# One visit of TensorE for the state products of two blocks, and a new order of seven output products

## The chip, the cores and the metric

The kernel runs on one core of a Trainium2 chip. Its time is device microseconds of one execution; of several executions the median counts. TensorE (PE) multiplies and writes its products to PSUM, which has eight banks of 128x512 float32. VectorE (DVE) and ScalarE (ACT) read the banks out, GpSimd (POOL) works on SBUF alone, and SyncE (SP) issues every DMA. PEld is the weight load that goes ahead of each matmul.

## The reference

Attention between 512 tokens and 32 state rows for 8 batches (blocks) of 8 heads, in both directions, and then two gated layers on 4608 tokens of width 512 with 1536 hidden features, all in float32:

```python
a = softmax(x @ state.T / 8);  xread = a @ state       # per block and head, D = 64
a2 = softmax(state @ x.T / 8); sread = a2 @ x
x = concat(xread, sread) as [4608, 512]
x = ((x @ w_a) * (x @ w_b)) @ w_out                    # layer 1
x = (silu(x @ w_gate) * (x @ w_val)) @ w_out2          # layer 2
```

## The kernel before

**Arithmetic.** A float32 operand is split into a high part and a rest (`hi_lo`, L355: a cast on ACT, a subtraction on DVE), and a product takes three matmuls: high by high, high by low, low by high. The attention weights `a` are not multiplied by the state first. The kernel multiplies the state by the layer's weights (`sw_here`, L512: state @ w) and then `a` by that, so a block needs state @ w for each of six column groups `fp`. One such product is a *visit*: eight matmuls of 64 rows by 32 columns (two heads in the row halves, four head pairs in the column strips), which the chip runs as sixteen records, eight at a time. Its two banks are then split into `swh` and `swl` (L526 to L529).

**Stages.** Blocks 0 to 3 start layer 1 alone or in pairs; then the pairs (0,1), (2,3), (4,5), (6,7) follow in `pair` (L803), and the rows of the states (`moe("s")`). For each feature group, `gemm` (L707, matmuls at L713) makes two products into the banks `ab0` and `ab1`; one is copied out (L344), the other multiplied onto it (L962). The product with `w_out` for a pair of blocks is done by seven products in place of eight (Winograd's scheme). Their operands are sums made on DVE (`operand_sums`), and the products 1, 2, 6, 5, 7, 4, 3 are *units*, one for each half i of the columns (`unit`, matmuls at L1120). A unit has two running banks, X for the products 1, 6, 7, 4 and Y for 2, 5, 3. After each product the running sum is copied out of its bank (`c`, added to `acc` from an earlier chunk), so the next product on that bank has to wait for the copy. In layer 1, X0 and X1 are the banks `po2` and `po3`, Y0 and Y1 are `po0` and `po1`. Layer 2 (`second`) uses the same scheme for its gate and value products (L954) and its output units; its weights are converted in the time of layer 1, kept in DRAM, and loaded again `AHEAD_US["w"]` ahead of use (tiles `wg`, `w2`, `w1`, `wv`).

**Order.** Everything is recorded as tasks (`Program.add`) with engines, an estimated cost, buffers, a due time and sometimes an earliest start. `Program.order` is a list scheduler that writes one order for all engines: a free engine takes the ready task that is due first. Tasks of `main` (the big products) carry a planned clock; the tasks on PE without one are the visits: scores `psc` (L562), transposes `pr`, `pat` and `pa` (L580, L626, L660), reads `psr` (L679, 64 records), `pst` (L694) and state @ w (L522). Visits other than the first take their banks from two spare banks, tag `pt`. Forty-four *warm* tasks fill planned gaps of PE early on. The kernel has one SP queue for every DMA. The numbers at the top (starts, leads, due times, room) set where the tasks fall.

Of the kernel before, what the change touches and what calls it, by code (L numbers as in the profile page):

```python
# [10 lines left out]
F32 = mybir.dt.float32  # L11
# [25 lines left out]

FIRST_US = 30.013
STRETCH = (1.317, 1.675)

# [3 lines left out]

LEAD = (110.0, 45.724, 24.087)
ATT = (70.0, 168.526)
# [5 lines left out]

DUE = (4.03, 14.955, 38.625, -19.901, 92.0, 5.114)

# [3 lines left out]
HERE = 6  # L58
LOAD_US = 8.393
# [12 lines left out]

SPARE_US = 0.229

RESERVE, FAR_US = {"w": 3, "h": 6, "pt": 0}, 37.297
ROOM = {"w": 41, "h": 24, "pt": 2}

# [4 lines left out]
PASS_US, HALF_PASS_US = 0.2267, 0.12  # L82
SWITCH_US = 0.2
HOP_US, PE_HOP_US = 0.25, 0.3
# [9 lines left out]
def dve(n, fast=False):  # L94
    a, b = FAST_US if fast else DVE_US
    return {"DVE": a + b * n}


# [25 lines left out]
class Program:  # L124
# [37 lines left out]
    def order(self):  # L162
# [18 lines left out]
        wire = 0.0  # L181
        shared = 0.0
        events = []

# [8 lines left out]
        while events:  # L193
# [18 lines left out]
            for e, heap in ready.items():  # L212
                if free[e] > now + 1e-9:
                    continue
                held = []
                blocked = shared > now + 1e-9 and e in ("DVE", "POOL")
                while heap:
                    item = heapq.heappop(heap)
# [22 lines left out]
                    us = t.engines[e] * (2.0 if e == "PE" and t.engines[e] < 1.0 and now < COLD_US else 1.0)  # L241
                    free[e] = end = now + us
# [30 lines left out]
class Kernel:  # L273
# [238 lines left out]
    def sw_here(self, b, fp, start):  # L512

        w, st = self.whole(b, fp, start - LOAD_US), self.own_state(b)
        banks = FIRST_BANKS if b == fp == 0 else (None, None)
        ps = [self.bank(f"sw{b}_{fp}_{h}", banks[h]) for h in range(2)]

        def fn(pe):
# [4 lines left out]

        self.pe(4 * PASS_US + SWITCH_US, fn, [st, *(buf for buf, _ in w)], ps, start=start)
        hi, lo = self.w_buf(f"swh{b}_{fp}"), self.w_buf(f"swl{b}_{fp}")
# [22 lines left out]
    def attention(self, b, start, span, by_x, by_s):  # L548
# [17 lines left out]
        for h in range(2):  # L566
# [3 lines left out]
            parts.append(self.softmax2(b, h, sT, by_s))  # L570
        self.reads(b, parts, by_s)
        return out

    def turned(self, b, h, sT, by):
# [6 lines left out]

        self.pe(0.44, turn, [sT, self.ident], [ps], by=by)
        return ps

    def softmax1(self, b, g, scores, by):
# [34 lines left out]
        if scores.psum:  # L620
# [6 lines left out]

            self.pe(0.44, turn, [sn, self.ident], [pt], **kw)
            return self.split(f"xs{nm}", pt, psum=True, **kw)
# [4 lines left out]
    def softmax2(self, b, g, sT, by):  # L634
# [20 lines left out]
        self.vec(150, second, [], [st], **kw)  # L655
        pa = self.bank(f"pa{nm}")

        def turn(pe):
            for c in range(4):
                pe.transpose(pa.t[:, c * P:(c + 1) * P], e2.t[:, c * P:(c + 1) * P], self.ident.t)  # L660

        self.pe(0.44, turn, [e2, self.ident], [pa], **kw)
        xn = self.load(self.w_buf(f"xn{nm}", F32, (1024,)), self.xn[b, g], P * 4096, start=by - 25)
        a2 = self.h_buf(f"a2{nm}")
        self.copy(lambda: a2.t, lambda: pa.t, 512, [pa], [a2], **kw)
        return a2, xn, st

    def reads(self, b, parts, by):
# [15 lines left out]

        self.pe(1.1 + SWITCH_US, fn, [t for a2, xn, _ in parts for t in (a2, xn)], [ps], **kw)
        sr = self.h_buf(f"sr{b}")
# [86 lines left out]
    def out_s_part(self, f, hs, po):  # L773
# [3 lines left out]
        self.dma(  # L777
            lambda: w.t.bitcast(F32), lambda: wt.t[:, slice(0, 8, 7) if f % 2 == 0 else slice(1, 7, 5)], [wt], [w],
            P * 4096, start=self.clock - AHEAD_US["t"] * self.stretch
# [23 lines left out]
    def pair(self, u, v, xs, ws, lo, hi):  # L803
# [37 lines left out]
        ck = dict(u=u, v=v, lo=lo, n=chunk, made=made, last=hi == NFP, step=1)  # L841
        self.units = [(ck, q, i) for q in (1, 2, 6, 5, 7, 4, 3) for i in range(2)]

    def second_weights(self, f, start):
# [19 lines left out]
        if f % 2 == 0:  # L864
            self.even = t, o
            return
        self.keep_combined(f"{f // 2}", *self.even, t, o, self.wt[f // 2])

    def keep_combined(self, nm, te, e, t, o, d):
        c3, c4 = self.combined(nm, te, e, t, o)  # L870
        for k, (buf, of), at in (
            ("e", ((te, 0), e), slice(0, 8, 7)), ("o", ((t, 0), o), slice(1, 7, 5)),
            ("3", (c3, lambda: c3.t), slice(2, 4)), ("4", (c4, lambda: c4.t), slice(4, 6))
        ):
# [24 lines left out]
    def first_combined(self, fp, wo, start):  # L899
        d, raw = self.wt1[fp], []  # L900
        for f in (2 * fp, 2 * fp + 1):
            b, of = self.h_buf(f"wof{f}"), self.wof[f]
            self.dma(lambda b=b: b.t, lambda of=of: of.t, [of], [b], P * 2048, start=start)
            raw += [b, lambda b=b: b.t]
            for slot, c in ((f % 2, slice(0, 256)), (7 - f % 2, slice(256, 512))):
                self.dma(
# [3 lines left out]
        c3, c4 = self.combined(f"f{fp}", *raw)  # L910
        for k, c, at in (("3", c3, slice(2, 4)), ("4", c4, slice(4, 6))):
            self.kept(f"wt1{k}{fp}", c, lambda c=c: c.t, d, lambda x, at=at: x[:, at], lambda t: t)
# [59 lines left out]
    def second(self, u, v, ops, xs_s, chunk):  # L972
# [3 lines left out]
        for lo in range(0, NFP, chunk):  # L976
# [60 lines left out]
            ck = dict(u=u, v=v, lo=lo, n=chunk, made=made, last=last, step=2)  # L1037
            self.units = [(ck, q, i) for q in (1, 2, 6, 5, 7, 4, 3) for i in range(2)]
            if xs_s:
# [39 lines left out]
    def unit(self):  # L1079
# [8 lines left out]
        wt = self.wt1 if ck["step"] == 1 else self.wt  # L1088
        ahead = lambda k: self.clock - AHEAD_US[k] * self.stretch
        if i == 0:  # L1090
            at = (1, 2, 6, 5, 7, 4, 3).index(q)
            if at % 2 == 0:
# [133 lines left out]
    def body(self):  # L1226
# [58 lines left out]
        for fp in range(NFP):  # L1285
# [19 lines left out]
            for f in (2 * fp, 2 * fp + 1):  # L1305
# [5 lines left out]
                if f % 2:  # L1311
                    self.keep_combined(f"f{fp}", *wo1[f - 1], *wo1[f], self.wt1[fp])
        ws, sw, xs_s = {}, {}, []
        self.acc, self.units = {}, []
        for blk, lo, hi in order:
# [10 lines left out]
            if blk == "s":  # L1326
# [15 lines left out]
                continue  # L1342
            of = {}
            for b in blk if isinstance(blk, tuple) else (blk,):
                for fp in range(lo // 2, hi // 2):
                    sw[b, fp] = self.sw(b, fp, begin[b, 2 * fp] - LEAD[2])
                of[b] = self.weights(
# [93 lines left out]
```

## Time and profile before

| | |
|---|---|
| median of 3 runs | 1413.85 us (1412.05 to 1415.42) |
| the profiled execution | 1416.01 us, its span 1414.2 us |
| PE busy | 1403.5 us, 99% of the span |
| DVE busy | 1097.2 us, 78% |
| ACT busy | 722.1 us, 51% |
| granted clock of PE | 1.00 in the mean of the span |

A busy PE does not tell how fast its stream goes: matmuls overlap, and the profile's 390 ns of one 128x512 matmul is a latency. Their starts, 0.23 us apart, are the rate. What a visit costs is read from starts too: from the last matmul before it to the first after it.

### The profile page before, as it was taken

To read this page: it belongs to the slowest core of one execution; us is meant where nothing else is said; L and a number is where in the kernel's file an instruction comes from. 1 tells how busy PE (TensorE), PEld (TensorE's weight loads), DVE (VectorE), ACT (ScalarE), POOL (GpSimd) and SP (SyncE) were. 2 spreads that over 40 slices of the span, in tenths; PEclk is the share of its full clock that TensorE was granted. 3 is DMA by queue.
4 is the path that set the end of the run, shared out by engine and by line. 5 is a ranking of instruction groups with operands and counts; after the bars stand their busy time and mean duration, and the time that the engine had idled before them with its cause. 6 is when DMAs were issued, how large, how long until landed. Compare 5 with 4: busy or idle time off the path is not lost.

```text
span 1414.2 us, 21772 instructions
## 1 busy us (share of the span) xinstructions
PE 1403.5 (99%) x7676; PEld 1120.6 (79%) x7676; DVE 1097.2 (78%) x1911; ACT 722.1 (51%) x1331; POOL 101.7 (7%) x78
## 2 busy tenths in 40 slices
PE   9999999999999999999999999999999999999998
PEld 7777777766777777899888788888888888888887
DVE  7999999998999998978787986649655595545464
ACT  7777675546565657556456633335323362333350
POOL 2222120000111011001011000000000000000000
PEclk9999999999999999999999999999999999999999
DMA  9879987977768898999998996668856686456486
GB/s 363 283 267 346 341 324 263 334 259 257 255 216 273 313 315 296 335 383 344 399 323 328 338 370 222 232 215 265 308 183 227 245 296 233 163 209 247 157 265 225
DMA packets 153932, 396.50 MB, mean 280 GB/s; under 512 B 16352, under 2 KB 20448, under 8 KB 153824
## 3 DMA queue, kind: packets, MB, share of 16 engines
q1 hardware_dynamic: 153824, 395.12, 79.5%
q8 instruction: 61, 1.00, 0.3%
q14 instruction: 47, 0.39, 0.1%
HBM read 298.06 MB, written 96.99 MB: 279 GB/s over the span
## 4 chain that ended last, share of the span: by engine, by line
PE 71%; DMA 3%; DVE 1%; ACT 1%; issue 0%; SPq 0%; DVEq 0%
PE pu L1120 24%; PE pX L954 18%; PE pC L954 9%; PE p L713 8%; PE pY L954 4%; PE p_s L713 2%; PE sw L522 1%; DMA w<-w 1%; PE po_s L789 1%; PE pvs L713 1%; PE pgs L713 1%; PE pus L1178 1%; DMA raw_o<-in_wo 1%; DMA xn<-in_xn 0%; DMA accc<-c 0%; DMA raw_v<-in_wab 0%
## 5 line engine op out<-in xcount | busy, mean ns | idle before, releaser
L1120 PE MATMUL pu<-S,wt 128*128 128x512 f32 x1932 | 472.5, 392 | 0.0
L1120 PEld LDWEIGHTS pu<-S,wt 128*128 128x128 f32 x1932 | 358.7, 188 | 98.1 <-issue 21.0
L713 PE MATMUL p<-xs,swh 128*128 128x512 f32 x768 | 242.5, 397 | 4.3 <-ACT a L344 2.0
L954 PE MATMUL pX<-x,w 128*128 128x512 f32 x864 | 219.9, 390 | 1.0 <-ACT t L344 0.5
L954 PEld LDWEIGHTS pX<-x,w 128*128 128x128 f32 x864 | 161.5, 188 | 35.6 <-ACT t L344 1.4
L713 PEld LDWEIGHTS p<-xs,swh 128*128 128x128 f32 x768 | 140.3, 188 | 53.3 <-ACT a L344 5.9
L713 PE MATMUL p<-xs,swl 128*128 128x512 f32 x384 | 149.9, 390 | 0.0
L962 DVE TENSOR_TENSOR t<-t,pC 128x512 f32<-128x512 f32 x96 | 65.9, 686 | 100.9 <-ACT t L344 87.6
L344 ACT COPY t<-pX 128x512 f32<-128x512 f32 x77 | 45.1, 586 | 101.7 <-PE pX L954 94.7
L352 DVE TENSOR_TENSOR S<-S,S 128x512 fp32r<-128x512 f32 x138 | 90.3, 694 | 3.4 <-ACT S L359 3.3
L962 DVE TENSOR_TENSOR c<-c,pu 128x512 f32<-128x512 f32 x102 | 69.6, 685 | 24.9 <-PE pu L1120 18.2
L344 ACT COPY a<-p 128x512 f32<-128x512 f32 x77 | 45.2, 587 | 84.7 <-PE p L713 53.8
L359 ACT CAST S<-S 128x512 fp32r<-128x512 f32 x138 | 78.9, 622 | 13.1 <-DVE S L962 5.4
L713 PEld LDWEIGHTS p<-xs,swl 128*128 128x128 f32 x384 | 72.1, 188 | 15.7
L962 DVE TENSOR_TENSOR c<-acc,pu 128x512 f32<-128x512 f32 x80 | 54.8, 686 | 28.8 <-PE pu L1120 22.8
L954 PE MATMUL pC<-x,w 128*128 128x512 f32 x288 | 73.1, 389 | 0.0
L954 PE MATMUL pX<-x,wg 128*128 128x512 f32 x282 | 71.7, 390 | 0.0
L954 PE MATMUL pC<-x,wv 128*128 128x512 f32 x282 | 71.6, 389 | 0.0
L954 PE MATMUL pY<-x,wg 128*128 128x512 f32 x282 | 71.6, 389 | 0.0
L968 ACT ACTIVATE c<-c 128x512 f32<-128x512 f32 x48 | 30.3, 631 | 72.8 <-DVE c L962 72.7
L359 ACT CAST swh<-sw 128x512 fp32r<-128x512 f32 x96 | 51.7, 589 | 28.9 <-PE sw L522 20.5
L352 DVE TENSOR_TENSOR swl<-sw,swh 128x512 fp32r<-128x512 f32 x96 | 61.8, 684 | 5.6 <-ACT swh L359 4.6
(203 smaller groups left out, 2132.1 us busy)
## 6 DMA issues: line engine op xcount, KB each, us to landing
wt<-wt SPq DMA_DIRECT2D x154, 512.0 KB, 6.3
w<-w SPq DMA_DIRECT2D x118, 512.0 KB, 6.4
wg<-w2g SPq DMA_DIRECT2D x47, 512.0 KB, 5.5
w1l<-wf SPq DMA_DIRECT2D x72, 256.0 KB, 5.1
accc<-c SPq DMA_DIRECT2D x72, 256.0 KB, 4.1
acc<-accc SPq DMA_DIRECT2D x72, 256.0 KB, 5.4
raw_w<-in_wab SPq DMA_DIRECT2D x24, 512.0 KB, 6.5
wt<-wt SPq DMA_DIRECT2D x46, 256.0 KB, 5.1
```

The lines of the kernel that those rows point to most:

```text
L344: self.nc.scalar.copy(out(), in_())
L352: lambda e: self.by_engine[e].tensor_tensor(out=out(), in0=in0(), in1=in1(), op=ALU.subtract), r, w, **kw
L359: self.p.add(act(n), lambda e: self.nc.scalar.copy(hi(), src()), [src_buf], [hb], **kw)
L522: pe.matmul(ps[h].t[cs], lhsT=st.t[rows, cs], rhs=of()[rows], start=True, stop=True)
L713: pe.matmul(ps.t[:, :n], lhsT=l, rhs=r, start=i == 0, stop=i == last)
L789: pe.matmul(ps.t[:, c], lhsT=w.t[:, k, hw, lc], rhs=hs.t[:, hh, :ST], start=f == i == j % 2 == 0, stop=f == NF - 1 and i == 2, skip_group_ ...
L954: pe.matmul(ps.t, lhsT=w.t[:, half, hw, i * P:(i + 1) * P], rhs=x.t[:, hx], start=start and i == n == 0, stop=stop and i == 1 and n == 2, ...
L962: self.vec(512, lambda e: e.tensor_tensor(out=to(), in0=a(), in1=b(), op=op), r, [w], **kw)
L968: self.p.add(act(n), lambda e: self.nc.scalar.activation(out=out.t[:, :n], in_=ps.t[:, :n], func=AF.Silu), [ps], [out])
L1120: pe.matmul(ps.t, lhsT=w.t[:, half, hw, c], rhs=x.t[:, hx], start=starts and k == m == 0, stop=stops and k == n - 1 and m == 2, skip_group ...
L1178: pe.matmul(ps.t, lhsT=h.t[:, hh, c], rhs=w.t[:, :, hw], start=k == m == 0, stop=k == len(hs) - 1 and m == 2)
```

## The change

The two blocks of a pair get state @ w in one PE task (`sw_both`), with four banks: two spare ones, and `po0` and `po1`. To free these, layer 1's units are ordered 1, 6, 7, 4, 2, 5, 3 and Y uses the same banks as X. The slots of the output weights in DRAM follow that order. The transposes `pa` of both parities (heads 0 and 1 of a pair) become one task. The scheduler prices the first visit after a main task, holds a lone visit back, and lets other visits that are due within 60 us join one that runs. Some twenty constants differ, among them the lead of layer 2's weights (21.73 to 12), the start of their conversion and the room for buffers.

```diff
-FIRST_US = 30.013
-STRETCH = (1.317, 1.675)
+FIRST_US = 31.986
+STRETCH = (1.318, 1.8)
...
-LEAD = (110.0, 45.724, 24.087)
+LEAD = (69.954, 54.422, 17.786)
...
-DUE = (4.03, 14.955, 38.625, -19.901, 92.0, 5.114)
+DUE = (5.0, 14.955, 40.0, -30.0, 40.0, 2.853)
...
-NEXT_US = 134.259
+NEXT_US = 119.329
...
-STAGGER = 40
-FROM_US = 252.5
-DIRECT = 11
-PACE = 1.062
-COMBOS = (75.0, 15.0)
+STAGGER = 49.629
+FROM_US = 305.45
+DIRECT = 12
+PACE = 0.909
+COMBOS = (100.0, 17.68)
 HELD = 4
-AHEAD_US = {"t": 18.453, "s": 10.342, "acc": 5.741, "w": 21.73, "x": 35.19}
+AHEAD_US = {"t": 17.835, "s": 10.054, "acc": 5.741, "w": 12, "x": 40}
...
-ROOM = {"w": 41, "h": 24, "pt": 2}
+ROOM = {"w": 40, "h": 26, "pt": 2}
...
-SWITCH_US = 0.2
+SWITCH_US, VISIT_US, JOIN_US, HOLD_US = 0.14, 0.2, 60.0, 10.0
...
+ORDER = {1: (1, 6, 7, 4, 2, 5, 3), 2: (1, 2, 6, 5, 7, 4, 3)}
...
+                join = [
+                    q for q in heap if not (q[2].main or q[2].spare or q[2].engine is not None) and q[2].by < main + JOIN_US
+                ] if e == "PE" else []
+                join.sort(reverse=True)
+                alone = len(join) == 1 and not visiting
...
+                    if e == "PE" and alone and not (t.main or t.spare) and t.by > main + HOLD_US:
+                        held.append(item)
+                        continue
...
+    def sw_both(self, u, v, fp, start):
+
+        w, st = self.whole(u, fp, start - LOAD_US), [self.own_state(b) for b in (u, v)]
+        ps = [[self.bank(f"sw{b}_{fp}_{h}", h if b == v else None) for h in range(2)] for b in (u, v)]
+        parts = [self.state_products(s, w, p) for s, p in zip(st, ps)]
+
+        def fn(pe):
+            for part in parts:
+                part(pe)
+
+        self.pe(
+            8 * PASS_US + SWITCH_US, fn, [*st, *(buf for buf, _ in w)], [p for pair in ps for p in pair], start=start
+        )
+        return [self.sw_split(b, fp, p) for b, p in zip((u, v), ps)]
...
-        pa = self.bank(f"pa{nm}")
...
+    def turned2(self, b, parts, by):
+        pa = [self.bank(f"pa{b}_{g}") for g in range(2)]
...
-        half = (0, 1, 0, 1, 0, 1, 0)[(1, 2, 6, 5, 7, 4, 3).index(q)]
+        half = at % 2
         if q in (1, 2, 5):
             tag = f"X{i}" if q == 1 else f"Y{i}"
-            po = 2 + i if q == 1 else i if ck["step"] == 1 else None
+            po = 2 + i if q == 1 or ck["step"] == 1 else None
...
-        if q == 7:
+        if q == (5 if ck["step"] == 1 else 7):
...
+            for fp in range(lo // 2, hi // 2):
+                if isinstance(blk, tuple) and fp < HERE and (lo or fp):
+                    sw[blk[0], fp], sw[blk[1], fp] = self.sw_both(*blk, fp, begin[blk[0], 2 * fp] - LEAD[2])
+                    continue
+                for b in blk if isinstance(blk, tuple) else (blk,):
+                    sw[b, fp] = self.sw(b, fp, begin[b, 2 * fp] - LEAD[2])
```

The built programs show what this does to PE's order. The first place is state @ w of the column group 4 for the pair (2,3) (`sw2_4`, `sw3_4`; `p0_` are the main products, `pu1_` the units). Before, block 3 on PE:

```order
L713 MATMUL p0_2_9_1_3299<-xs2_1_855,swl2_4_3225 128x512
L522 MATMUL sw3_4_0_3316<-w1l2_4_0_2855,strt3_312 32x512
L522 MATMUL sw3_4_1_3317<-w1l2_4_0_2855,strt3_312 32x512
L522 MATMUL sw3_4_0_3316<-w1l2_4_1_2861,strt3_312 32x512
L522 MATMUL sw3_4_1_3317<-w1l2_4_1_2861,strt3_312 32x512
L522 MATMUL sw3_4_0_3316<-w1l2_4_2_2872,strt3_312 32x512
L522 MATMUL sw3_4_1_3317<-w1l2_4_2_2872,strt3_312 32x512
L522 MATMUL sw3_4_0_3316<-w1l2_4_3_2875,strt3_312 32x512
L522 MATMUL sw3_4_1_3317<-w1l2_4_3_2875,strt3_312 32x512
L1120 MATMUL pu1_0_4_2_0_3331<-S1_0_4_2_0_3185,wt1_0_4_1_4_3105 128x512 x3
```

It stands by itself; block 2's eight came 42 main matmuls earlier. After, on PE, the end of block 2's part and all of block 3's:

```order
L570 MATMUL sw2_4_0_3180<-w1l2_4_3_2989,strt2_284 32x512
L570 MATMUL sw2_4_1_3181<-w1l2_4_3_2989,strt2_284 32x512
L570 MATMUL sw3_4_0_3182<-w1l2_4_0_2930,strt3_329 32x512
L570 MATMUL sw3_4_1_3183<-w1l2_4_0_2930,strt3_329 32x512
L570 MATMUL sw3_4_0_3182<-w1l2_4_1_2936,strt3_329 32x512
L570 MATMUL sw3_4_1_3183<-w1l2_4_1_2936,strt3_329 32x512
L570 MATMUL sw3_4_0_3182<-w1l2_4_2_2939,strt3_329 32x512
L570 MATMUL sw3_4_1_3183<-w1l2_4_2_2939,strt3_329 32x512
L570 MATMUL sw3_4_0_3182<-w1l2_4_3_2989,strt3_329 32x512
L570 MATMUL sw3_4_1_3183<-w1l2_4_3_2989,strt3_329 32x512
L771 MATMUL p0_1_11_1_3207<-xs1_0_472,swh1_5_3001 128x512 x2
```

The two blocks follow each other with no main matmul between. The second place is the units of the pair (0,1), chunk 4. `S1_0_4_6_0` is the operand of product 6, and the two names that begin with `pu1_0_4_1` are X0 and X1. PE before:

```order
L1120 MATMUL pu1_0_4_2_0_3331<-S1_0_4_2_0_3185,wt1_0_4_1_4_3105 128x512 x3
L1120 MATMUL pu1_0_4_2_0_3331<-S1_0_4_2_1_3193,wt1_0_4_1_5_3160 128x512 x3
L1120 MATMUL pu1_0_4_2_1_3349<-S1_0_4_2_0_3185,wt1_0_4_1_4_3105 128x512 x3
L1120 MATMUL pu1_0_4_2_1_3349<-S1_0_4_2_1_3193,wt1_0_4_1_5_3160 128x512 x3
L1120 MATMUL pu1_0_4_1_0_3227<-S1_0_4_6_0_3234,wt1_0_4_6_4_3122 128x512 x3
L1120 MATMUL pu1_0_4_1_0_3227<-S1_0_4_6_1_3256,wt1_0_4_6_5_3173 128x512 x3
L713 MATMUL p0_3_8_0_3383<-xs3_0_953,swh3_4_3344 128x512 x2
```

Product 2 on its own bank stands between the products 1 and 6 of X0. PE after, at the products 6 and 7:

```order
L1179 MATMUL pu1_0_4_1_0_3345<-S1_0_4_6_0_3244,wt1_0_4_1_4_3260 128x512 x3
L1179 MATMUL pu1_0_4_1_0_3345<-S1_0_4_6_1_3274,wt1_0_4_1_5_3293 128x512 x3
L1179 MATMUL pu1_0_4_1_1_3359<-S1_0_4_6_0_3244,wt1_0_4_1_4_3260 128x512 x3
L1179 MATMUL pu1_0_4_1_1_3359<-S1_0_4_6_1_3274,wt1_0_4_1_5_3293 128x512 x3
L1179 MATMUL pu1_0_4_1_0_3345<-S1_0_4_7_0_3270,wt1_0_4_7_4_3326 128x512 x3
L1179 MATMUL pu1_0_4_1_0_3345<-S1_0_4_7_1_3308,wt1_0_4_7_5_3342 128x512 x3
L1179 MATMUL pu1_0_4_1_1_3359<-S1_0_4_7_0_3270,wt1_0_4_7_4_3326 128x512 x3
L1179 MATMUL pu1_0_4_1_1_3359<-S1_0_4_7_1_3308,wt1_0_4_7_5_3342 128x512 x3
```

X0 comes again after one unit of six matmuls on X1.

## Rows read from the trace of the kernel before

**Rows 1.** The page's head: span; busy time of each engine.
```profile
span 1414.2 us, 21772 instructions
PE 1403.5 (99%) x7676; PEld 1120.6 (79%) x7676; DVE 1097.2 (78%) x1911; ACT 722.1 (51%) x1331; POOL 101.7 (7%) x78
```
**Rows 2.** Waits of PE: total us, times, longest; first and last listed.
```profile
PE p L713 <- ACT a L344: 2.0, 3, 1.2
...
PE p L713 <- DVE ve L962: 0.3, 1, 0.3
```
**Rows 3.** Windows: busy us of PE, PEld, DVE, ACT, POOL; clock; DMA share, GB/s.
```profile
250.00:350.00 100.00, 96.33 (x573) 68.69 (x572) 91.22 (x171) 52.24 (x99) 2.81 (x2) 1.00 0.82 280
350.00:650.00 300.00, 299.59 (x1880) 233.73 (x1879) 275.05 (x493) 183.28 (x346) 32.81 (x23) 1.00 0.86 299
```
**Rows 4.** Groups by line: state @ w, its two forms.
```profile
L522 PE MATMUL sw<-w1l,strt 64*32 64x512 f32 x576 | 40.1, 601 | 0.0
L522 PE MATMUL sw<-cv_w,strt 64*32 64x512 f32 x192 | 13.2, 601 | 0.0
```
**Rows 5.** Timeline of PE, one visit: start us, us, what.
```profile
292.05 0.62 PE L713 MATMUL p<-xs,swh 128*128 128x512 f32 x2
292.52 0.39 PE L713 MATMUL p<-xs,swl 128*128 128x512 f32 x1
292.83 1.09 PE L522 MATMUL sw<-w1l,strt 64*32 64x512 f32 x16
293.85 0.72 PE L713 MATMUL p<-xs,swh 128*128 128x512 f32 x2
294.42 0.40 PE L713 MATMUL p<-xs,swl 128*128 128x512 f32 x1
```
**Rows 6.** Timeline of PE, reads of one block, then of two together.
```profile
127.56 1.10 PE L679 MATMUL psr<-xn,a 128*32 128x64 f32 x64
128.59 0.73 PE L713 MATMUL p<-xs,swh 128*128 128x512 f32 x2
...
167.51 1.99 PE L679 MATMUL psr<-xn,a 128*32 128x64 f32 x128
169.44 0.33 PE L694 MATMUL pst<-ident,sr 128*128 128x128 f32 x1
```
**Rows 7.** Timeline of PEld: the weight loads of the visit in Rows 5.
```profile
292.83 0.18 PEld L522 LDWEIGHTS sw<-w1l,strt 64*32 64x32 f32 x16 [0.36 <-issue]
```
**Rows 8.** Timeline of DVE: the rests of that visit's banks.
```profile
297.32 1.29 DVE L352 TENSOR_TENSOR swl<-sw,swh 128x512 fp32r<-128x512 f32 x2 [1.96 <-ACT swh L359]
```
**Rows 9.** Timeline: PE's first matmul behind a unit, DVE's copy of it; three times.
```profile
229.57 0.62 PE L713 MATMUL p<-xs,swh 128*128 128x512 f32 x2
229.77 0.69 DVE L962 TENSOR_TENSOR c<-acc,pu 128x512 f32<-128x512 f32 x1
...
268.71 0.70 PE L713 MATMUL p<-xs,swh 128*128 128x512 f32 x2
...
270.99 0.65 DVE L962 TENSOR_TENSOR c<-acc,pu 128x512 f32<-128x512 f32 x1
...
298.08 0.61 PE L713 MATMUL p<-xs,swh 128*128 128x512 f32 x2
...
302.60 0.69 DVE L962 TENSOR_TENSOR c<-acc,pu 128x512 f32<-128x512 f32 x1
```
**Rows 10.** Timeline of DVE: a reduction of the softmax.
```profile
267.34 0.68 DVE L609 TENSOR_REDUCE sm<-sn 128x16 f32<-128x512 f32 x1
```
**Rows 11.** Gate weights: first issue (SP), first use (PE), landing from 650 to 690.
```profile
657.50 0.33 SPq L333 DMA_DIRECT2D wg<-w2g  x1
...
671.32 1.55 PE L954 MATMUL pX<-x,wg 128*128 128x512 f32 x6
...
DMA to landing us min/median/max: 6.1/8.1/10.0
```
**Rows 12.** The page's DMA issues: bytes of one, median us to landing.
```profile
w<-w SPq DMA_DIRECT2D x118, 512.0 KB, 6.4
```

More of the change, by code (lines that the diff above doesn't have):

```diff
@@ L96, in dve @@
     return {"DVE": a + b * n}
+ORDER = {1: (1, 6, 7, 4, 2, 5, 3), 2: (1, 2, 6, 5, 7, 4, 3)}
+SLOTS = {
+    k: {"e": slice(0, 8, 7), "o": slice(o.index(2), 7, o.index(3) - o.index(2)),
+        "3": slice(o.index(6), o.index(5) + 1, o.index(5) - o.index(6)),
+        "4": slice(o.index(7), o.index(4) + 1, o.index(4) - o.index(7))}
+    for k, o in ORDER.items()
+}
 class Buf:
@@ L182, in order @@
         shared = 0.0
+        visiting = False
         events = []
@@ L216, in order @@
                 blocked = shared > now + 1e-9 and e in ("DVE", "POOL")
-                while heap:
-                    item = heapq.heappop(heap)
+                join = [
[3 more added lines that the diff above has]
+                alone = len(join) == 1 and not visiting
+                if not visiting:
+                    join = []
+                while heap:
+                    if join:
+                        item = join.pop()
+                        heap.remove(item)
+                        heapq.heapify(heap)
+                    else:
+                        item = heapq.heappop(heap)
                     t = item[2]
@@ L241, in order @@
                     us = t.engines[e] * (2.0 if e == "PE" and t.engines[e] < 1.0 and now < COLD_US else 1.0)
+                    if e == "PE":
+                        visit = not (t.main or t.spare)
+                        us += VISIT_US * (visit and not visiting)
+                        visiting = visit
                     free[e] = end = now + us
@@ L516, in sw_here, with state_products @@
         ps = [self.bank(f"sw{b}_{fp}_{h}", banks[h]) for h in range(2)]
+        self.pe(4 * PASS_US + SWITCH_US, self.state_products(st, w, ps), [st, *(buf for buf, _ in w)], ps, start=start)
+        return self.sw_split(b, fp, ps)
+    def sw_both(self, u, v, fp, start):
[9 more added lines that the diff above has]
+        return [self.sw_split(b, fp, p) for b, p in zip((u, v), ps)]
+    def state_products(self, st, w, ps):
         def fn(pe):
@@ L522, in fn, with sw_split @@
                     pe.matmul(ps[h].t[cs], lhsT=st.t[rows, cs], rhs=of()[rows], start=True, stop=True)
-        self.pe(4 * PASS_US + SWITCH_US, fn, [st, *(buf for buf, _ in w)], ps, start=start)
+        return fn
+    def sw_split(self, b, fp, ps):
         hi, lo = self.w_buf(f"swh{b}_{fp}"), self.w_buf(f"swl{b}_{fp}")
@@ L570, in attention @@
             parts.append(self.softmax2(b, h, sT, by_s))
-        self.reads(b, parts, by_s)
+        self.reads(b, self.turned2(b, parts, by_s), by_s)
         return out
@@ L580, in turn @@
                 pe.transpose(ps.t[:, r], sT.t[:, r], self.ident.t)
-        self.pe(0.44, turn, [sT, self.ident], [ps], by=by)
+        self.pe(0.4, turn, [sT, self.ident], [ps], by=by)
         return ps
@@ L626, in turn @@
                     pe.transpose(pt.t[:, r], sn.t[:, r], self.ident.t)
-            self.pe(0.44, turn, [sn, self.ident], [pt], **kw)
+            self.pe(0.4, turn, [sn, self.ident], [pt], **kw)
             return self.split(f"xs{nm}", pt, psum=True, **kw)
@@ L655, in softmax2 @@
         self.vec(150, second, [], [st], **kw)
-        pa = self.bank(f"pa{nm}")
+        xn = self.load(self.w_buf(f"xn{nm}", F32, (1024,)), self.xn[b, g], P * 4096, start=by - 25)
+        return e2, xn, st
+    def turned2(self, b, parts, by):
+        pa = [self.bank(f"pa{b}_{g}") for g in range(2)]
         def turn(pe):
[L659 to L666, printed above, removed]
+            for (e2, _, _), ps in zip(parts, pa):
+                for c in range(4):
+                    r = slice(c * P, (c + 1) * P)
+                    pe.transpose(ps.t[:, r], e2.t[:, r], self.ident.t)
+        self.pe(0.8, turn, [self.ident, *(e2 for e2, _, _ in parts)], pa, by=by)
+        out = []
+        for g, (ps, (_, xn, st)) in enumerate(zip(pa, parts)):
+            a2 = self.h_buf(f"a2{b}_{g}")
+            self.copy(lambda a2=a2: a2.t, lambda ps=ps: ps.t, 512, [ps], [a2], by=by)
+            out.append((a2, xn, st))
+        return out
     def reads(self, b, parts, by):
@@ L683, in fn @@
                         )
-        self.pe(1.1 + SWITCH_US, fn, [t for a2, xn, _ in parts for t in (a2, xn)], [ps], **kw)
+        self.pe(0.88 + SWITCH_US, fn, [t for a2, xn, _ in parts for t in (a2, xn)], [ps], **kw)
         sr = self.h_buf(f"sr{b}")
@@ L777, in out_s_part @@
         self.dma(
-            lambda: w.t.bitcast(F32), lambda: wt.t[:, slice(0, 8, 7) if f % 2 == 0 else slice(1, 7, 5)], [wt], [w],
+            lambda: w.t.bitcast(F32), lambda: wt.t[:, SLOTS[1]["eo"[f % 2]]], [wt], [w],
             P * 4096, start=self.clock - AHEAD_US["t"] * self.stretch
@@ L841, in pair @@
         ck = dict(u=u, v=v, lo=lo, n=chunk, made=made, last=hi == NFP, step=1)
-        self.units = [(ck, q, i) for q in (1, 2, 6, 5, 7, 4, 3) for i in range(2)]
+        self.units = [(ck, q, i) for q in ORDER[1] for i in range(2)]
     def second_weights(self, f, start):
@@ L904, in first_combined @@
             raw += [b, lambda b=b: b.t]
-            for slot, c in ((f % 2, slice(0, 256)), (7 - f % 2, slice(256, 512))):
+            at = SLOTS[1]["eo"[f % 2]]
+            for slot, c in ((at.start, slice(0, 256)), (at.stop - 1, slice(256, 512))):
                 self.dma(
@@ L1037, in second @@
             ck = dict(u=u, v=v, lo=lo, n=chunk, made=made, last=last, step=2)
-            self.units = [(ck, q, i) for q in (1, 2, 6, 5, 7, 4, 3) for i in range(2)]
+            self.units = [(ck, q, i) for q in ORDER[2] for i in range(2)]
             if xs_s:
@@ L1089, in unit @@
         ahead = lambda k: self.clock - AHEAD_US[k] * self.stretch
+        at = ORDER[ck["step"]].index(q)
         if i == 0:
-            at = (1, 2, 6, 5, 7, 4, 3).index(q)
             if at % 2 == 0:
```

18 lines of the change are left out of this document (8 added, 10 removed).

## The prediction, written before the changed kernel was run

> **What bounds the kernel now.** I read the page's head, PE's waits, the stretches, and then the timeline of PE at single visits. The head shows PE busy for 1403.5 of 1414.2 us, DVE next with 78% [rows 1]. A busy PE could still be slow, so the waits come second: six, 4.9 us in all without the one at the start, the largest group 2.0 us and the smallest 0.3 us, all behind copies and sums of ACT and DVE [rows 2]. PE's stream thus sets the end, and what leaves it shortens the kernel unless a new wait stands in its place. The candidate for that is DVE: 91.2 of 100 us from 250 to 350 us, 275.1 of 300 from 350 to 650 [rows 3], which is where the changed part lies. The first of these is also the stretch in which PE was idle most, 3.7 us.
>
> Both programs hold the same matmuls; DVE has three rows fewer of 1913. What differs is how often PE leaves its main stream, and how closely one order follows another.
>
> **Merged visits.** State @ w has 768 records [rows 4], sixteen to a visit, so 48 visits. One stands in rows 5. Two main matmuls start 0.47 us apart over two steps (292.05 to 292.52), so one step is 0.235. From the last main start before the visit to the first after it is 293.85 - 292.52 = 1.33. The two matmuls behind it then take 294.42 - 293.85 = 0.57 where 0.47 is usual, 0.10 more. The visit costs 1.33 - 0.235 + 0.10 = 1.20 us.
>
> What a second block adds inside the same visit is not in the trace. The sixteen records last 1.09 us together and 0.60 each [rows 4, 5], so the last starts 0.49 after the first; eight records start within some 0.04, which leaves 0.45 from one set of eight to the next. Two more sets are 0.90. The nearest row that shows a doubled visit agrees: the reads of one block occupy PE from 127.56 to 128.59, 1.03 us, those of two from 167.51 to 169.44, 1.93 us, again 0.90 for the second [rows 6]. So a merge saves 1.20 - 0.90 = 0.30 us. The bounds are nothing (two full visits after all) and the 0.30 itself, since sets cannot come closer than in rows 5; I take 0.30. The built program has 19 merged visits and 10 single ones: 19 x 0.30 = **-5.7 us**.
>
> The loads of the second block's states are part of that price. All sixteen loads of a visit stand within 0.18 us of its start [rows 7], while its first eight matmuls run until 0.60, so the loads of the second eight went in under matmuls of the same row halves. The Trainium skill, "TensorE: Matmul & The Clock Gate", section Part 3 on row and column tiling, says that a weight load overlaps matmuls in flight only where the row group differs; by it each merge would pay 0.18 again and the term would be 19 x 0.12 = -2.3 us. The trace shows otherwise for this form, so I stay with the row.
>
> **Other visits.** In PE's order 82 visits become 61: 19 by these merges, one by the transposes, one in the start-up, among warm matmuls. Seven of the eight blocks had both transposes `pa` side by side already. The one that is new is worth 0.3 at most; I count nothing.
>
> **Slack behind a visit.** The rests of the visit in rows 5 were done at 297.32 + 1.29 = 298.61, 4.8 us after PE left it [rows 8]. Counting PE's rows by their durations, the first reader of `swl` followed a visit by less than 4 us at 10 of 48 places before, and at 3 after; the median goes from 4.5 to 6.0 us. The transposes' readers move from 1.4 to 2.7 us at three blocks. This should give back part of the 4.9 us of waits; ends 0 and -4.9, and I take **-1.5**. The four banks of a merged visit have to be split by ACT and DVE as before, no more of them in all.
>
> **Banks that come back sooner.** This is the price of the new unit order. A unit may not start on X or Y until the running sum is copied out. Counted the same way, layer 1 has 72 such returns; before, the closest came 4.1 us behind the end of the last unit on its bank and 6 came within 6 us; now four come after 1.36 us (one unit of six steps), three after 2.7, two after 3.8, and 26 within 6. The copy is done 230.46 - 229.57 = 0.9 us behind the unit where DVE is free, 271.64 - 268.71 = 2.9 us where it is behind, and 303.29 - 298.08 = 5.2 us at worst shown [rows 9]. At 0.9 no return waits. At 2.9 the four nearest wait 1.54 each and the next three 0.2: 6.9 us. At 5.2 four wait 3.8, three 2.5, two 1.4 and some 12 more up to a microsecond: about 35 us, and behind a waiting unit stands everything else on PE. In DVE's new order the copies of the closest group (products 6 and 7) have mostly one other instruction between them, such as a reduction of 0.68 us [rows 10]: with the copy 1.37 against the 1.36 of a unit, just in step, plus two short ones. Nearest is the case of 0.9; for the short ones and a late start at two places I take **+1.5**, ends 0 and +35.
>
> **Layer 2's weights.** Their lead falls from 21.73 to 12. In the built list the first gate weights stand 6.5 us of PE work ahead of use before and 2.2 after, the second 5.2 and 2.7. In the trace the first were issued at 657.50 and used at 671.32, 13.8 us ahead, and landing there took 8.1 us in the median, 10.0 at worst [rows 11]. With 4.3 us less, 9.5 us are left: enough for the median, 0.5 short at worst. I take **+0.5**, ends 0 and +4 (four loads, each 1 us late). Later on some 12 us of plan stand against 6.4 us of landing [rows 12]; no wait.
>
> **The rest.** The number of warm matmuls is the same, and two more of them stand ahead of the first main product (60 for 58), so the start-up counts nothing, with 2 us either way for its other order. The last unit and its output are unchanged.
>
> Sum: -5.7 - 1.5 + 1.5 + 0.5 = -5.2 us. The profiled execution took 1416.0 us, of it 1414.2 in the span, and lies 2.2 above the median of 1413.85. So 1416.0 - 5.2 = 1410.8 for an execution like the profiled one, and **1408.6** for the median.
>
> **Rivals.**
>
> *The returns wait (slower).* The new order puts PE behind DVE's copies of the running sums, at the group of products 6 and 7 of pair (0,1) and at pair (2,3)'s first chunk. If these copies come 3.5 us behind their units, between the 2.9 and the 5.2 of rows 9, four returns wait 2.14 and three 0.8: 10.9 us in place of 1.5. The sum is then +4.2 and the time 1418. It decides from a copy 2.9 us late, where it cancels the gain. For it: both rows of late copies stem from that very chunk, in the stretch with DVE at 91% [rows 3]. Against it: DVE's order now has the copies directly behind the units.
>
> *DVE sets the pace (no change).* All merges lie in the time of layer 1, where DVE has 92% [rows 3]. If its work and not PE's decided there, the 5.7 us would turn into waits and the time stay at 1413.9. Against it: 24.9 us of DVE were idle from 350 to 650, and PE waited less than 0.5 there. The Trainium skill says on this, in "TensorEngine Tiling (Array Packing)", section PSUM Bottleneck, that tiling speeds up TensorE but not the evacuation of PSUM, so that the copies may become the bottleneck; the rows above show DVE near it but not at it.
>
> *Late weights (no change).* The loads at the start of layer 2 cost the upper end, 4 us, in place of 0.5: -1.7, 1412.1.
>
> *The waits go as well (faster).* The looser splits remove all of the 4.9 us of waits, with 0.10 for the slower second step behind each of six, and no new ones come: -5.7 - 5.5 = -11.2, 1402.6.
>
> **How the numbers follow.** What a measurement can tell here is about 0.2%, 2.8 us: faster is below 1411.0, slower above 1416.7. The forecast has 0.50 (its own range 1405 to 1411), the waits that go 0.12: faster 0.62. DVE's pace 0.12 and the late weights 0.10: no change 0.22. The returns 0.16: slower. The range runs from 1402, which takes in most of the faster rival, to 1417, the nearer part of the slower one.
>
> **What would show it.** In the changed kernel's profile, a visit of 32 records of state @ w should take some 1.99 us, 2.23 between main starts, with 61 runs of visits; 2.4 from main start to main start or more says that merging saves little. Waits of `pu` on a copy `c` near 270 us tell the returns, waits of `pX` or `pY` on `wg`, `w2` or `w1` near 660 us the late weights; both together should stay under 2 us. Waits of `p` should fall below 4.9 us. The prediction is wrong if PE's waits grow by more than they lost in visits.

## The result and the profile after

The changed kernel takes 1402.33 us in the median of six runs (1401.76 to 1404.10), the kernel before 1414.31 in the same comparison: ratio 0.9918, 95% interval 0.9906 to 0.9931, or 12.0 us less. The forecast was 5.2 us less; the time is the one that the rival *the waits go as well* gave. The head and PE's waits after:

```profile
span 1402.2 us, 21751 instructions
PE 1392.5 (99%) x7676; PEld 1125.2 (80%) x7676; DVE 1095.8 (78%) x1908; ACT 722.6 (52%) x1334; POOL 101.9 (7%) x78
```

```profile
PE p L771 <- ACT a L373: 1.9, 1, 1.9
PE warm L1299 <- POOL ident masks.py:199: 1.4, 1, 1.4
PE sw L570 <- DVE swl L381: 1.1, 1, 1.1
PE p L771 <- DVE U L1021: 0.6, 1, 0.6
PE pX L1013 <- ACT t L373: 0.4, 1, 0.4
PE pst L752 <- ACT sr L747: 0.2, 1, 0.2
```

The span is 12.0 us shorter and PE's busy time 11.0 [rows 1]: part of that is visits, part delays that a busy PE hides. The waits without the start's are 4.2 us, hardly less than the 4.9 of before [rows 2]. The list misleads here: 1.3 of the 4.2 stand inside visits (`sw`, `pst`), and a wait is listed from a matmul's modelled end, 0.39 us after its start, while the next could have started after 0.23, so each is 0.16 longer than it reads. I therefore added up the distances from start to start on PE, by what stood there. Of a difference of 12.1 us, 5.4 are at the visits with the step behind them (92.0 to 86.6; 6.4 to 6.9 once the waits inside visits are taken out, 0.6 to 1.1 before and 2.1 after, by where one draws the line), 6.2 are delays between main matmuls (3.9 of them in *late steps*, more than 0.13 us late, whose sum went from 7.3 to 3.4; 1.1 in the second step behind each, 0.11 slower, at 13 places before and 3 after; the rest in small ones), and 0.5 at warm matmuls. The windows tell where the second part lies: PE's busy time from 250 to 350 us went from 96.33 [rows 3] to 99.79.

```profile
250.00:350.00 100.00, 99.79 (x675) 73.74 (x674) 98.39 (x182) 52.20 (x100) 5.41 (x4) 1.00 0.91 322
350.00:650.00 300.00, 297.48 (x1840) 239.28 (x1839) 274.02 (x492) 185.83 (x351) 31.30 (x22) 1.00 0.89 314
```

A merged visit on PE (start, duration, what), and its weight loads:

```profile
322.70 1.32 PE L1179 MATMUL pu<-S,wt 128*128 128x512 f32 x5
323.95 1.95 PE L570 MATMUL sw<-w1l,strt 64*32 64x512 f32 x32
325.83 0.74 PE L771 MATMUL p<-xs,swh 128*128 128x512 f32 x2
326.41 0.40 PE L771 MATMUL p<-xs,swl 128*128 128x512 f32 x1
```

```profile
323.95 0.18 PEld L570 LDWEIGHTS sw<-w1l,strt 64*32 64x32 f32 x16 [0.36 <-issue]
324.41 0.15 PEld L570 LDWEIGHTS sw<-w1l,strt 64*32 64x32 f32 x8 [0.28 <-issue]
324.84 0.15 PEld L570 LDWEIGHTS sw<-w1l,strt 64*32 64x32 f32 x8 [0.28 <-issue]
```

From its first record to the next main matmul it takes 1.88 us (325.83 - 323.95), where a visit of 16 records takes 1.02 [rows 5]. Over all undisturbed visits, counted as in the prediction from start to start with the slower step behind, the median is 2.079 us for a merged one and 1.219 for a single one, so a merge saves 2 x 1.219 - 2.079 = 0.36, and 19 of them 6.8 us.

### The profile page after: what moved, and what is told of

Same layout as the page of the kernel before. It is cut to its first block, busy times and chain, and to the rows that moved or that the text cites. A ratio compares the mean times of both kernels' runs of the same rounds, so it can differ in the third digit from the quotient of the medians.

```text
span 1402.2 us, 21751 instructions
## 1 busy us (share of the span) xinstructions
PE 1392.5 (99%) x7676; PEld 1125.2 (80%) x7676; DVE 1095.8 (78%) x1908; ACT 722.6 (52%) x1334; POOL 101.9 (7%) x78
## 4 chain that ended last, share of the span: by engine, by line
PE 72%; DMA 2%; DVE 1%; ACT 1%; issue 0%; SPq 0%; ACTq 0%; DVEq 0%
PE pu L1179 24%; PE pX L1013 18%; PE pC L1013 9%; PE p L771 7%; PE pY L1013 5%; PE p_s L771 2%; PE sw L570 1%; PE po_s L847 1%; PE pvs L771 1%; PE pgs L771 1%; PE pus L1237 1%; DMA raw_v<-in_wab 1%; DMA raw_g<-in_wab 1%; DMA w2g<-w2g 1%; DMA w1l<-wf 0%; ACT sg L447 0%
## 5 line engine op out<-in xcount | busy, mean ns | idle before, releaser
L373 ACT COPY a<-p 128x512 f32<-128x512 f32 x82 | 48.2, 588 | 88.2 <-PE p L771 85.7
L1027 ACT ACTIVATE gv<-pX 128x512 f32<-128x512 f32 x48 | 28.7, 598 | 69.4 <-PE pX L1013 69.3
L381 DVE TENSOR_TENSOR S<-U,S 128x512 fp32r<-128x512 f32 x92 | 60.8, 695 | 3.6 <-ACT S L388 3.4
```

The source lines that it names most:

```text
L373: self.nc.scalar.copy(out(), in_())
L381: lambda e: self.by_engine[e].tensor_tensor(out=out(), in0=in0(), in1=in1(), op=ALU.subtract), r, w, **kw
L1027: self.p.add(act(n), lambda e: self.nc.scalar.activation(out=out.t[:, :n], in_=ps.t[:, :n], func=AF.Silu), [ps], [out])
```

## The experiments

Each number is the median, and the ratio to the kernel before that ran beside it (its median was 1412.6 to 1414.2); 0.001 is 1.4 us. Four theories: *slack* (waits went because merged visits leave more time), *order* (because of the products' new order), *numbers* (because of the retuned numbers, above all when layer 2's weights are converted), and *fit* (numbers are tuned to one order, and any other order has other waits).

**First: parts of the change.** No merged visits:

```diff
-if isinstance(blk, tuple) and fp < HERE and (lo or fp):
+if isinstance(blk, tuple) and False:
```

> The changed kernel with no merged visits: each block's state @ w is its own visit again; the new order of products, the banks, the joined transposes and the new numbers stay. Measured so far: before 1414.3, changed 1402.3; PE's start-to-start times put 5.7 of the 12.0 us at the visits and 6.2 at waits that are gone. All theories: the visits cost some 5.7 us again. Slack (the waits went because the rests of a merged visit are split with more time to spare): the waits come back too, 1414. Numbers (they went because the retuned numbers move the conversions and loads out of 250 to 350 us) and order (they went because of the new order of the products, which changes what stands in DVE's queue ahead of an eviction): the waits stay away, 1408, and waits of p stay under 3 us.

1412.97, ratio 1.0000 (0.9990 to 1.0010): 11.6 us lost, more than the 6.8 of the visits. By the total this is what *slack* expects. The trace speaks against it: PE's waits of `p`, which *slack* said would come back, stay away.

```profile
PE sw L570 <- DVE swl L381: 1.9, 1, 1.9
PE warm L1299 <- POOL ident masks.py:199: 1.4, 1, 1.4
PE pX L1013 <- ACT t L373: 1.3, 1, 1.3
PE pu L1179 <- DMA wt<-wt: 0.8, 2, 0.7
PE p L771 <- ACT a L373: 0.6, 1, 0.6
```

Its late steps add up to 2.8 us, the changed kernel's to 3.4. What its profiled execution lost, 8.2 us of span, stands at the visits: their price, and waits in front of them. One visit PE enters 2.1 us late, on PE's timeline:

```profile
94.75 0.40 PE L771 MATMUL p<-xs,swl 128*128 128x512 f32 x1
97.09 1.68 PE L570 MATMUL sw<-w1l,strt 64*32 64x512 f32 x16 [1.95 <-DVE swl L381]
98.71 0.50 PE L771 MATMUL p<-xs,swh 128*128 128x512 f32 x1
```

It waits for the split `swl` of an earlier visit, which still holds a spare bank; three more visits, near 195, 245 and 289 us, run 0.4 to 0.7 over.

All fourteen numbers of before in the changed kernel, and all fourteen new ones in the kernel before:

```diff
-FROM_US = 305.45
+FROM_US = 252.5
...
-ROOM = {"w": 40, "h": 26, "pt": 2}
+ROOM = {"w": 41, "h": 24, "pt": 2}
```

> The changed kernel with the fourteen numbers of before that it also had (leads, due times, start and pace of the conversions, buffers): merged visits, order of products and joined transposes stay. Slack and order: 1402 to 1403, as the changed kernel. Numbers: the merges keep their 5.7 us and the waits come back, 1408.5, with more than 4 us of waits of p and pX between 250 and 350 us.

> The kernel before with the fourteen numbers of the changed kernel and nothing else. Slack and order: 1414, as before. Numbers: the waits go, the visits stay, 1408.

The changed kernel with the old numbers: 1427.43, ratio 1.0099 (1.0083 to 1.0116), 14 us *slower* than before, with late steps of 18.9 us in all, at unlike places. No theory gave this: with the old numbers the new structure is a loss. The kernel before with the new numbers: 1411.00, ratio 0.9988 (0.9979 to 0.9996). Its late steps fall from 7.3 to 3.4 us, as *numbers* expects, but its visits take 1.8 us more than before, and the total falls short of the 1408 that it expected.

Without merges and with the old order of the products (the edit also takes back the banks of Y and the merges):

```diff
...
-ORDER = {1: (1, 6, 7, 4, 2, 5, 3), 2: (1, 2, 6, 5, 7, 4, 3)}
+ORDER = {1: (1, 2, 6, 5, 7, 4, 3), 2: (1, 2, 6, 5, 7, 4, 3)}
...
```

> The changed kernel without merged visits and with the old order of the seven products and Y in banks 0 and 1 again: what is left of the change is the numbers, the joined transposes and the planner's rule of joining. Slack and order: 1414. Numbers: 1408. Against the run without merges alone it tells what the order does by itself: equal by the theory of the numbers, 6 us slower by that of the order.

1410.02, ratio 0.9981 (0.9971 to 0.9991): 2.7 us faster than with the new order. So the order does not remove waits; *order* falls. By itself, without merges, it is no gain.

**Second: how much is fit, and is it slack?** A number moved by a meaningless amount, in the changed kernel and in the run without merges; and a longer lead for single visits:

```diff
-FROM_US = 305.45
+FROM_US = 304.45
```

> The changed kernel with one number moved by a meaningless amount: the conversions start at 304.45 in place of 305.45 us of plan. The planner's greedy order comes out otherwise in hundreds of places, the structure is the same. Slack (merged visits leave few waits whatever the details): 1402 to 1404, ratio to before 0.992 as the changed kernel. Fit (the numbers were searched for this one order, and its few waits are that search's): some waits come back, 1405 to 1410, ratio 0.994 to 0.998, PE's stalls over the changed kernel's 3.4 us, at places with nothing in common.

> The run without merged visits, with the same meaningless nudge. Slack: 1413 again, 11 us behind the nudged changed kernel. Fit: anywhere from 1409 to 1417, and only about 6 us behind the nudged changed kernel, which is what the visits are worth.

```diff
-LEAD = (69.954, 54.422, 17.786)
+LEAD = (69.954, 54.422, 24.087)
```

> The run without merged visits, with each visit planned 24.1 us ahead of its weights' first use, as before, in place of 17.8. Slack: if single visits lacked time behind them, this gives it back: waits of sw and p on swl and evictions go, 1408. Fit: no such return, 1410 to 1416.

In this order: 1405.01, ratio 0.9938 (0.9925 to 0.9951); 1414.78, 1.0006 (0.9996 to 1.0016); 1414.99, 1.0008 (1.0000 to 1.0017). One microsecond in one number cost the changed kernel 2.8 us: that much of the 12.0 belongs to this one order. The longer lead gave nothing back, and without merges the waits of `p` stayed away (0.6 us, and 1.4 in its nudged twin), so *slack*, my reason in the prediction, falls. Undoing the merges costs 11.6 us, and 9.6 between the nudged twins; some 4 of the mean are lost beside the visits' own price. In the first of these runs 2.1 came where a single visit waits for the spare bank of another, and the rest I did not test.

**Third: the conversions alone.** Their planned start, end and pace, moved in the kernel before and moved back in the changed one, each with a nudged twin (start 1 us earlier):

```diff
-NEXT_US = 134.259
+NEXT_US = 119.329
-FROM_US = 252.5
+FROM_US = 305.45
-PACE = 1.062
+PACE = 0.909
```

> The kernel before, with the conversions of layer 2's weights planned as in the changed kernel (start 305.45 for 252.5 us, end and pace too) and all else as before. In before's trace PE stalls 4.6 us between 290 and 346 us, where ACT and DVE waited up to 5 us for loads. Numbers: with the conversions' loads out of that stretch these stalls go, 1409. Slack, order and fit: no gain beyond 1.5 us, or other stalls elsewhere, 1411 to 1417.

> The kernel before with the conversions' start at 251.5 in place of 252.5 us of plan. Numbers: 1412 to 1417, its waits between 290 and 346 us still there. Fit: anywhere from 1409 to 1418; at 1410 or less the gain of the late conversions would be no more than a lucky order.

> The kernel before with the late conversions, start at 304.45 in place of 305.45 us of plan. Numbers: 1408 to 1412, under the kernel before by 2 us or more. Fit: 1409 to 1418.

> The changed kernel with the conversions of layer 2's weights planned as before (start 252.5 us, end and pace of before) and all else as changed. Late conversions gave 4.4 us in the kernel before. Numbers, as a term of its own: the same 4.4 us are lost here, 1406.7, ratio to before 0.995. Fit: 1405 to 1412, no fixed sum. Slack: 1403.

> The run before this one with the start at 251.5 in place of 252.5 us of plan, a meaningless nudge. Numbers: within 3 us of that run, and both behind the changed kernel and its nudged twin. Fit: the four lie mixed.

| ratio to before | early conversions | late conversions |
|---|---|---|
| kernel before | 1 | 0.9969 (0.9957 to 0.9981) |
| its nudged twin | 0.9999 (0.9990 to 1.0007) | 0.9978 (0.9968 to 0.9989) |
| changed kernel | 0.9958 (0.9943 to 0.9973) | 0.9918 (0.9906 to 0.9931) |
| its nudged twin | 0.9962 (0.9947 to 0.9977) | 0.9938 (0.9925 to 0.9951) |

This is the answer, as *numbers* said in all five runs. By the means of the twins, late conversions give 0.0026 (3.7 us) in the old structure and 0.0032 (4.5 us) in the new one, each known to some 2 us by the intervals. The late steps agree: 7.3 and 6.4 us (twin) with early conversions and 2.6 and 2.5 with late ones in the old structure, 5.4 and 4.4 against 3.4 and 3.8 in the new one. All else of the change gives 0.0040 (5.6 us) with early and 0.0046 (6.4 us) with late conversions. That is near the 6.8 of the merged visits, but as a sum: the merges are worth 10.6 by the means of the two pairs above, so the rest of the change takes some 4 back. The two parts add up to 10.1 us, and the changed kernel's own order lies 1.4 better than its mean with its twin. Which of the three numbers does it was not separated, and with all fourteen the kernel before gains less than with these three. In the trace of the kernel before with late conversions, PE's waits and the window (busy 98.85 for 96.33 [rows 3]):

```profile
PE warm L1240 <- POOL ident masks.py:199: 1.4, 1, 1.4
PE p L713 <- DVE V L962: 1.2, 1, 1.2
PE p L713 <- ACT a L344: 0.5, 2, 0.4
```

```profile
250.00:350.00 100.00, 98.85 (x606) 71.60 (x604) 95.80 (x179) 52.70 (x99) 2.87 (x2) 1.00 0.79 268
```

**Fourth: how an early conversion costs PE anything.** The largest stall left in the changed kernel suggests a way, first on PE, then on ACT:

```profile
470.00 0.39 PE L771 MATMUL p<-xs,swl 128*128 128x512 f32 x1
472.28 0.72 PE L771 MATMUL p<-xs,swh 128*128 128x512 f32 x2 [1.90 <-ACT a L373]
```

```profile
465.54 2.03 ACT L388 CAST swh<-sw 128x512 fp32r<-128x512 f32 x4
469.92 0.66 ACT L432 ACTIVATE cv_g<-raw_g 128x512 f32<-128x512 f32 x1 [2.35 <-DMA raw_g<-in_wab]
470.49 0.76 ACT L447 ACTIVATE sg<-raw_g 128x512 f16<-128x512 f32 x1
471.12 0.64 ACT L435 ACTIVATE cv_g<-raw_g 128x512 int32<-128x512 uint32 x1
471.66 0.57 ACT L373 COPY a<-p 128x512 f32<-128x512 f32 x1
```

ACT stands for 2.35 us before a step that reads a raw load, two more conversion steps follow, and only then comes the copy `a` that frees PE's bank. The plan reckons with 2.2 us + 512 KB at 3.6e5 bytes per us = 3.7 us until such a load has landed; in this trace it takes 6.6 to 7.0 us in the median, from 300 to 650 us. So these steps stand too early in the queue: call this *queue*. The tests are known landings, in the kernel before and in the changed one with early conversions; more small buffers in the kernel before, against the rival that buffer slots are what is short (*slots*); and a still later start (340 us) in the changed kernel:

```diff
-end = max(wire, end) + DMA_US
+end = max(wire, end) + DMA_US + (3.5 if any(b.name[:5] in ("raw_g", "raw_v", "raw_o") for b in t.bufs) else 0)
```

> The kernel before, whose planner now reckons with 3.5 us more until a load of layer 2's raw weights has landed (the trace has 6 to 7 us, the plan 3.7), so that the steps reading it stand later in ACT's queue; the loads are issued as before. Queue (ACT stands still for these loads with evictions behind it): ACT's waits for raw loads go, PE's stalls from 290 to 346 us shrink, 1409 to 1410.5, ratio 0.997. Slots or traffic: 1412 to 1415.

> The changed kernel with the early conversions (1407.9, ratio 0.996), and the same 3.5 us more reckoned with. Queue: back to 1403 to 1405, ratio 0.993. Slots or traffic: 1407 to 1409.

```diff
-ROOM = {"w": 41, "h": 24, "pt": 2}
+ROOM = {"w": 40, "h": 26, "pt": 2}
```

> The kernel before with 40 large and 26 small buffers, as the changed kernel has, in place of 41 and 24. Slots (ACT waits up to 5 us for a small buffer that a store still reads): those waits shorten and PE's stalls near 302 to 314 us go, 1409 to 1411. Queue or traffic: 1412 to 1415.

> The changed kernel with the conversions from 340 us of plan on in place of 305.45. If early conversions cost by crowding the time before 350 us, most is gained already: 1401 to 1404. If each one costs wherever it stands closer together, the rest of layer 1 gets denser and it is slower: 1404 to 1408. Fit alone: 1403 to 1408.

The edit does what it is meant to do: from 250 to 650 us ACT's waits for raw loads fall from 25.5 us to 0.2 in the changed kernel with early conversions, and from 9.8 to nothing in the kernel before. The first went to 1403.70, ratio 0.9937 (0.9925 to 0.9950), as *queue* said: 0.0021 back, 3.0 us, though a nudge moves as much and this run has no twin. The kernel before became slower, 1416.05, 1.0026 (1.0015 to 1.0037), a miss by the total. In the stretch at issue 4.6 us of late steps from 290 to 346 became 0.3, and the window is full. But the last output weights of layer 2 are stored later (issued at 804.4 us for 796.9), and the start of layer 2 now waits for such weights:

```profile
250.00:350.00 100.00, 99.84 (x612) 72.82 (x611) 96.58 (x176) 58.40 (x109) 7.50 (x5) 1.00 0.89 310
```

```profile
PE pu L1120 <- DMA wt<-wt: 3.2, 2, 2.3
```

More slots: 1411.63, ratio 0.9992 (0.9984 to 1.0001), between what *slots* and its rivals said, and no clear gain. The stalls from 290 to 346 went here too, and others came (2.4 us in a visit at 117 us). The waits of ACT, then of DVE, in the kernel before from 285 to 346 us: stores that still read a small buffer, and loads of `acc`, came before raw loads:

```profile
ACT a L344 <- DMA x<-c: 8.3, 2, 5.0
ACT a L344 <- DVE c L962: 5.1, 1, 5.1
```

```profile
DVE c L962 <- DMA acc<-accc: 2.4, 1, 2.4
DVE swl L352 <- ACT swh L359: 2.4, 2, 2.0
```

Three different edits took most or all of the 4.6 us out of that stretch: 1.3 were left with late conversions, 0.3 with known landings and none with more slots, where the nudge alone left 4.3. So no single wait can be named as the cause; which of them an early conversion sets off in the kernel before stays open. Later still: 1406.76, ratio 0.9961 (0.9948 to 0.9975), 0.0043 or 6 us worse than the changed kernel. In its trace are 2.0 us of `pX` on `wg` at 813 us. That fits conversions that end late: their last step on ACT starts at 779.8 us for 769.5. The rest is spread over other late steps, or not seen in that execution.

**Last: both prices at once.** The known landings in the changed kernel, with its own start and with 280 us:

> The changed kernel, whose planner reckons with 3.5 us more until a raw load of layer 2's weights has landed. Queue alone: the waits of p near 444 and 472 us shrink, 1399 to 1401. Trade (steps later in the queue finish the conversions later, and layer 2's start waits for its weights): 1403 to 1408, with new waits between 750 and 830 us.

> The same with the conversions' start at 280 us of plan, between the two kernels. Trade: the best of the three starts with known landings, 1400 to 1403. Queue alone: equal to the run with the start of 305. Fit: anywhere from 1400 to 1407.

1401.60, ratio 0.9914 (0.9899 to 0.9929), just above what *queue* said and below *trade*; and 1399.93 (1399.15 to 1400.31), ratio 0.9900 (0.9883 to 0.9916): the fastest of all, and by the medians the best of the three starts, as *trade* said. The intervals of the two overlap with each other and with the changed kernel's. The stall at 472 us is gone in both. But ACT's waits for raw loads (250 to 650 us) had been 24.0 us in the changed kernel, more than twice the 9.8 of the kernel before, and taking them down to 0.2 brought no gain that can be told from noise. So ACT's standing still for these loads is not, by itself, what early conversions cost. The largest group of these waits in the changed kernel, and the only one left with known landings:

```profile
ACT cv_g L432 <- DMA raw_g<-in_wab: 11.8, 6, 4.1
```

```profile
ACT sg L447 <- DMA raw_g<-in_wab: 0.2, 1, 0.2
```

The second run, with the start at 280 us, has only these waits of PE left:

```profile
span 1398.5 us, 21750 instructions
```

```profile
PE warm L1299 <- POOL ident masks.py:199: 1.4, 1, 1.4
PE sw L570 <- DVE swl L381: 0.8, 1, 0.8
PE p L771 <- ACT a L373: 0.6, 1, 0.6
```

## Why the prediction was right in one half and wrong in the other

**Merged visits, -5.7: right, a little small.** 6.8 by the visits; 5.6 to 6.4 by the runs, with the rest of the structure. The single visit was priced at 1.20 and is 1.219; the second block at 0.90 and is 0.86, since the later sets of eight follow 0.43 us apart, not 0.45. So the bound of the prediction, that sets cannot come closer than in [rows 5], was wrong, by little. The loads, too: sixteen went in at once, and the other two sets of eight each 0.28 us after, while the eight matmuls before them (0.59 us each) still ran on the same row halves. The sentence of the Trainium skill ("TensorE: Matmul & The Clock Gate", Part 3) that a load overlaps matmuls in flight only where the row group differs would, taken alone, have left 2.3 us of the gain; the trace stands against it here.

**Slack behind a visit, -1.5: this step failed.** PE's waits did fall, by 6.2 us with their trailing steps, but not through looser splits: the waits removed were for the banks of `p`, not for `swh` or `swl`; they stayed away when the merges were undone, and longer leads without merges gave nothing. The largest single one in the kernel before is listed under DVE's `s`, but it ends where DVE's product `V` has read the bank (313.50 + 0.67 = 314.17):

```profile
313.50 0.67 DVE L962 TENSOR_TENSOR V<-a,p 128x512 f32<-128x512 f32 x1
```

```profile
314.23 0.73 PE L713 MATMUL p<-xs,swh 128*128 128x512 f32 x2 [1.32 <-DVE s L652]
```

The prediction took the waits as a by-product of the visits and never priced the one part of the diff that moved work into and out of the stretch where PE was idle most: `FROM_US`, `NEXT_US` and `PACE`. That stretch, 250 to 350 us, was named [rows 3], and the old start of 252.5 us is its left edge. Alone these numbers gave 3.1 to 4.4 us in the kernel before, and took its late steps from 7.3 to 2.6. How an early conversion comes to hold PE up stays open. The end of that term, 4.9 [rows 2], was too small as well: it took the listed waits for the whole delay, which was 7.3 in the late steps alone.

**Banks that come back sooner, +1.5: nothing.** No wait of `pu` on a copy is in the changed trace, though DVE was busy for 98.39 of those 100 us. The closest group stands in one row of PE, four units of six matmuls, 1.36 us each; DVE's copies of the first two:

```profile
273.46 5.66 PE L1179 MATMUL pu<-S,wt 128*128 128x512 f32 x24
```

```profile
275.22 0.67 DVE L1021 TENSOR_TENSOR c<-acc,pu 128x512 f32<-128x512 f32 x1
276.77 0.63 DVE L1021 TENSOR_TENSOR c<-acc,pu 128x512 f32<-128x512 f32 x1
```

The units on those banks start again at 276.18 and 277.54, so the copies were done 0.29 and 0.14 us ahead: just in step, as the prediction said. The danger was real: with the old numbers a unit waited 1.9 us for such a copy, near 243 us. That the order costs something by itself (2.7 us between the two runs without merges) is within what one order differs from the next.

**Layer 2's weights, +0.5: nothing.** The first were issued at 651.0 and used at 660.3, 9.3 us ahead for the 9.5 of the estimate; landing took 7.0 in the median and 9.4 at worst. Such loads did make PE wait in other runs: 4.1 us with the old numbers, 2.0 with the later start, 1.0 with the nudge. The shorter lead is not shown as their cause, since the first of these runs has the old lead of 21.73.

**The rivals.** *The waits go as well* had the right time, 1402.6, and a wrong cause, looser splits. That is luck: its visits were 1.1 us too small and its reason for the waits did not hold. *DVE sets the pace* was wrong, with DVE at 98% where the gain fell. *The returns wait* and *late weights* did not happen.

## What to carry to other kernels

In a kernel whose order a planner writes, a retuned number is an edit like any other: ask of each which instructions and loads it moves, and whether they leave or enter the stretch in which the bounding engine waits. Before a few microseconds are put down to a mechanism, nudge a number that means nothing: here one microsecond of plan moved the time by up to 2.8 us, so that one run with a part undone tells less than two by two runs with twins. And a step that waits for a load holds up what stands behind it on its engine, as ACT's copy at 471.66 shows. To plan such steps by the landing time of the trace took ACT's waits away, but it moved work later as well: with it one kernel gained 3.0 us, one lost 3.7, and in the changed kernel nothing clear came of it.

## What the runs showed of the hardware

Some stalls of PE cost more than their length. With the old numbers PE waited 4.1 us for a load at 820 us, and then its clock was granted at 0.50, the lower of its two levels, 1.2 GHz, for twelve matmuls, each start 0.43 us after the last in place of 0.23: 2.4 us more.

```profile
820.00:824.00 4.00, 0.06 (x1) 0.00 (x0) 4.00 (x8) 2.80 (x5) 0.00 (x0) 0.77 0.99 316
824.20:829.00 4.80, 4.80 (x12) 3.75 (x13) 4.80 (x9) 2.80 (x6) 0.00 (x0) 0.50 1.04 407
829.20:833.00 3.80, 3.80 (x18) 3.11 (x17) 2.34 (x5) 0.33 (x1) 0.00 (x0) 1.00 1.03 377
```

With early conversions seven matmuls were slowed in this way after a stall of 2.1 us at 496; in the changed kernel, after the 2.1 us at 470, none were:

```profile
498.40:502.40 4.00, 4.00 (x11) 3.19 (x12) 4.00 (x8) 1.10 (x2) 0.00 (x0) 0.61 0.73 292
```

```profile
474.00:478.00 4.00, 4.00 (x23) 3.27 (x21) 3.59 (x6) 4.00 (x8) 1.80 (x2) 1.00 1.01 386
```

Other stalls of that length went either way: eight matmuls were slowed after the 1.9 us near 243 with the old numbers (granted clock 0.57 from 245 to 249), seven after the 2.3 us near 816 with known landings in the kernel before (0.64 from 818.3 to 823), and none after the 2.0 us at 813 with the later start (1.00). So among these the length of the stall does not tell which are followed by slow matmuls.
